# A fused attention kernel on one core: first scores on 256 tokens, keys ahead of values, a longer ring at first, and output weights loaded in pieces

## The chip, the cores and the metric

The kernel runs on one core of one Trainium2 chip. The metric is the device time of one execution in microseconds (us). A profiled execution gives a trace, whose span is about 1 to 2 us shorter than the time. Short names of the engines: PE is TensorE (matmuls), PEld its weight loads, ACT is ScalarE, DVE is VectorE, POOL is GpSimd, SP is SyncE, which issues most DMAs here.

## The reference

Two attention blocks over 2048 tokens, width 1024, 32 heads of 32. Their outputs stand side by side.

```python
# A: softmax attention
q, k, v = split(A_x @ A_wqkv)                       # 32 heads x 2048 x 32
p = softmax(q @ k.T * 32 ** -0.5)                   # 2048 x 2048 for each head
a = (p @ v) @ A_wo
# B: four segments of 512 tokens; in a segment causal attention, mixed by a gate
# with a linear-attention memory M, z of the segments before
p = softmax(qs @ ks.T * scale + mask);  a_dot = p @ vs
a_mem = (phi(qs) @ M) / (phi(qs) @ z + 1e-6)
o = g * a_mem + (1 - g) * a_dot
M, z = M + phi(ks).T @ vs, z + sum(phi(ks))
b = o @ B_wo
return concatenate([a, b], -1)
```

## The kernel before

Everything is laid out at build time. A small list scheduler keeps its own estimate of the time of each engine, and emits instructions in the order in which it believes them to become ready. The order is then fixed: at run time each engine executes its list in order and waits on semaphores. The names that matter here:

- An **exponential** is one ACT instruction over 128 x 1024 scores (4 heads x 256 queries x 2 tiles of 128 keys make two of them). There are 1216.
- The **ring** PT holds exponentials until PE has multiplied them with V (**PV**) and with ones (the row sums).
- **Side work** of PE: projections of Q, K, V for the next heads, B's memory, output projections.
- **Filler matmuls**: while the scheduler's clock is under WARM = 60 us, it puts a dummy matmul wherever it sees PE idle for 0.15 us.

```python
SLOTS = [(0, 1), (2, 3), (4, 5)]     # PSUM banks of scores
RING = 20
PACE = 240                           # how early the projections of the next heads are made
WARM = 60
TURNS = 2                            # chunks of 512 tokens of x that PE transposes; the others by DMA
...
    def loads(self):
        for k in range(4 * TURNS):
            tile_in(k)               # 128 tokens of A's x, from the SP queue
            ...                      # the three weights go between
        for c in range(TURNS, 4):    # chunks 2 and 3: DMA transpose
            R.dma(... self.A_x[0][512 * c:512 * c + 512, :], transpose=True ...)
...
    def a_prep(self, g):             # K, Q, V of four heads
        for c in range(4):
            yield pace()
            yield from proj(0, c)                      # K of 512 tokens
            if early and c == 0:
                yield from proj(1, 0)                  # Q of 512 tokens
                self.events.add(("sA", g, 0))          # scores may start
                self.spawn(values(), (-1, 1.5), "valuesA0")    # V, between the keys
        ...
    def emit_pv(self, u, st, part):
        for ones in (False, True):
            for h in range(4):
                ...
...
            if now < WARM and gap >= 0.15:             # filler
                ...
                R.op("PE", lambda e, bank=spare[0]: e.matmul(self.ps[:, bank, :], self.ones[:, :], ...), cost=MM)
```

## Time and profile before

| | us |
|---|---|
| time, median of 3 runs (range) | 1177.57 (1177.24 to 1180.48) |
| span of the profiled run | 1177.4 |
| ACT busy | 1125.4 (96%) |
| of that, 1216 exponentials | 1103.2, so 0.907 each |
| PE busy | 1028.4 (87%) |

From the page of the kernel before: the busy time of each engine, then shares of 40 equal slices in tenths (PEclk is the granted TensorE clock, also in tenths), and the costliest group.

```profile
PE 1028.4 (87%) x16647; PEld 480.5 (41%) x16880; DVE 800.1 (68%) x1367; ACT 1125.4 (96%) x1256; POOL 116.1 (10%) x192
...
ACT  4899999999999999998999999999999999999994
...
PEclk9999999999999998997999999999999999899998
...
L538 ACT ACTIVATE PT<-ps 128x1024 bf16<-128x1024 f32 (+1 forms) x1216 | 1103.2, 1037 | 29.4 <-PE ps L512 27.2
```

ACT is full everywhere but in the first slices and the last. The clock row has 7s and 8s in the middle; the prediction below counts them as dips that may "fall elsewhere" and gives them no cause.

ACT's timeline of the kernel before (start, duration, engine, line, what, count, idle time before it and what ended that):

```profile
5.90 1.02 ACT L425 ACTIVATE xA<-ps 128x1024 bf16<-128x1024 bf16 x1 [3.62 <-PE ps L420]
8.95 1.02 ACT L425 ACTIVATE xA<-ps 128x1024 bf16<-128x1024 bf16 x1 [2.03 <-DVE xA L427]
16.44 7.49 ACT L538 ACTIVATE PT<-ps 128x1024 bf16<-128x1024 f32 x8 [6.46 <-PE ps L512]
25.69 1.94 ACT L538 ACTIVATE PT<-ps 128x1024 bf16<-128x1024 f32 x2 [1.76 <-PE ps L512]
28.63 1.94 ACT L538 ACTIVATE PT<-ps 128x1024 bf16<-128x1024 f32 x2 [1.00 <-PE ps L512]
32.43 2.85 ACT L538 ACTIVATE PT<-ps 128x1024 bf16<-128x1024 f32 x3 [1.86 <-PE ps L512]
...
40.60 18.52 ACT L538 ACTIVATE PT<-ps 128x1024 bf16<-128x1024 f32 x20 [1.65 <-PE ps L512]
```

The first exponential starts at 16.44 us; 18 are done at 40.6 us, where 24 more microseconds of work would have fitted. From then on ACT hardly pauses.

### The profile page before, as it was taken

To read this page: it belongs to the slowest core of one execution; us is meant where nothing else is said; L and a number is where in the kernel's file an instruction comes from. 1 tells how busy PE (TensorE), PEld (TensorE's weight loads), DVE (VectorE), ACT (ScalarE), POOL (GpSimd) and SP (SyncE) were. 2 spreads that over 40 slices of the span, in tenths; PEclk is the share of its full clock that TensorE was granted. 3 is DMA by queue.
4 is the path that set the end of the run, shared out by engine and by line. 5 is a ranking of instruction groups with operands and counts; after the bars stand their busy time and mean duration, and the time that the engine had idled before them with its cause. 6 is when DMAs were issued, how large, how long until landed. Compare 5 with 4: busy or idle time off the path is not lost.

```text
span 1177.4 us, 36953 instructions
## 1 busy us (share of the span) xinstructions
PE 1028.4 (87%) x16647; PEld 480.5 (41%) x16880; DVE 800.1 (68%) x1367; ACT 1125.4 (96%) x1256; POOL 116.1 (10%) x192
## 2 busy tenths in 40 slices
PE   8988988998898978888989887888998989799995
PEld 4444434443344434333444433434443434344442
DVE  4367477668877468768787777875868887854345
ACT  4899999999999999998999999999999999999994
POOL 1001010011111011102011111110111120200000
PEclk9999999999999998997999999999999999899998
DMA  7752133152311221411311123120131211200111
GB/s 170 149 123 47 33 73 67 41 109 42 73 28 33 56 51 38 82 38 28 73 51 34 33 56 68 29 55 20 42 70 33 51 42 29 82 28 20 38 38 66
DMA packets 203272, 65.92 MB, mean 56 GB/s; under 512 B 195938, under 2 KB 195938, under 8 KB 203106
## 3 DMA queue, kind: packets, MB, share of 16 engines
q1 hardware_dynamic: 203106, 63.46, 24.0%
q8 instruction: 134, 2.20, 0.8%
q14 instruction: 32, 0.26, 0.1%
HBM read 37.75 MB, written 8.39 MB: 39 GB/s over the span
## 4 chain that ended last, share of the span: by engine, by line
ACT 48%; PE 41%; DVE 7%; issue 2%; DMA 0%; SPq 0%; another core or an unknown queue 0%; DVEq 0%
ACT PT L538 46%; PE ps L685 22%; PE ps L587 11%; PE ps L512 8%; DVE SQ L610 2%; DVE OL L597 1%; ACT E L878 1%; DVE OL L645 0%; DMA OTA<-in_A_x_dram 0%; DVE amem L912 0%; DVE outsb L981 0%; DVE OTA L614 0%; DVE KQB L695 0%; DVE KA L695 0%; SPq L383 0%
## 5 line engine op out<-in xcount | busy, mean ns | idle before, releaser
L538 ACT ACTIVATE PT<-ps 128x1024 bf16<-128x1024 f32 (+1 forms) x1216 | 1103.2, 1037 | 29.4 <-PE ps L512 27.2
L587 PE MATMUL ps<-PT,ones 128*32 128x256 bf16 x4864 | 293.7, 275 | 0.0
L587 PE MATMUL ps<-PT,VA 128*32 128x256 bf16 x4096 | 252.8, 279 | 14.8 <-ACT PT L538 10.4
L512 PE MATMUL ps<-QA,KA 32*128 32x256 bf16 x4096 | 209.3, 277 | 43.6 <-ACT PT L538 37.1
L610 DVE RECIPROCAL SQ<-OL 128x128 f32<-128x128 f32 x256 | 242.8, 949 | 5.0
L685 PE MATMUL ps<-xB,WB 128*128 128x512 bf16 x689 | 177.1, 381 | 25.2 <-issue 11.2
L685 PE MATMUL ps<-xA,WA 128*128 128x512 bf16 x689 | 181.2, 389 | 15.3 <-issue 9.4
L558 POOL TENSOR_SCALAR_AFFINE_SELECT PT<-PT 128x512 bf16<-128x512 bf16 x128 | 85.1, 667 | 909.9 <-ACT PT L538 905.3
L512 PEld LDWEIGHTS ps<-QA,KA 32*128 32x128 bf16 x4096 | 61.6, 92 | 223.8 <-ACT PT L538 205.4
L587 PEld LDWEIGHTS ps<-PT,VA 128*32 128x32 bf16 x4096 | 109.0, 96 | 104.6 <-issue 66.2
L587 PEld LDWEIGHTS ps<-PT,ones 128*32 128x32 bf16 x4864 | 131.7, 98 | 2.8
L597 DVE COPY OL<-ps 128x512 f32<-128x512 f32 x128 | 85.7, 669 | 25.2 <-PE ps L587 23.7
L685 PEld LDWEIGHTS ps<-xB,WB 128*128 128x128 bf16 x768 | 62.2, 97 | 98.5 <-issue 46.4
L685 PEld LDWEIGHTS ps<-xA,WA 128*128 128x128 bf16 x768 | 63.4, 99 | 91.4 <-issue 29.8
L905 DVE RECIPROCAL den<-den 128x128 f32<-128x128 f32 x96 | 91.1, 949 | 2.1
L984 DVE CAST outsb<-ps 128x512 bf16<-128x512 f32 x56 | 38.5, 687 | 74.5 <-PE ps L685 74.4
L695 DVE CAST KQB<-ps 128x512 bf16<-128x512 f32 x64 | 43.6, 681 | 53.5 <-PE ps L685 53.0
L685 PE MATMUL ps<-xA,OTA 128*128 128x512 bf16 x231 | 61.0, 391 | 4.1 <-issue 3.8
L685 PE MATMUL ps<-WoB,OTB 128*128 128x512 bf16 x228 | 57.9, 380 | 7.4 <-issue 3.6
L645 DVE SCALAR_TENSOR_TENSOR OL<-OL,SQ 128x256 f32<-128x256 f32 x128 | 59.1, 462 | 4.4
L587 PE MATMUL ps<-PT,VB 128*32 128x256 bf16 (+1 forms) x768 | 48.0, 270 | 13.7 <-DVE OL L597 9.9
L695 DVE CAST QA<-ps 128x512 bf16<-128x512 f32 x32 | 22.1, 691 | 42.9 <-PE ps L685 42.6
(69 smaller groups left out, 488.2 us busy)
## 6 DMA issues: line engine op xcount, KB each, us to landing
WB<-in_B_wk_dram SPq DMA_DIRECT2D x32, 256.0 KB, 2.9
WB<-in_B_wq_dram SPq DMA_DIRECT2D x32, 256.0 KB, 2.9
WB<-in_B_wv_dram SPq DMA_DIRECT2D x32, 256.0 KB, 3.1
out_dram<-outsb SPq DMA_DIRECT2D x32, 256.0 KB, 2.0
WA<-in_A_wqkv_dram SPq DMA_DIRECT2D x24, 256.0 KB, 3.7
OTA<-in_A_x_dram SPq DMA_DIRECT2D x8, 256.0 KB, 4.9
WoB<-in_B_wo_dram SPq DMA_DIRECT2D x1, 2048.0 KB, 10.7
xA<-in_A_wo_dram SPq DMA_DIRECT2D x1, 2048.0 KB, 9.6
```

The costliest lines, as they stand in the source:

```text
L512: ins = e.matmul(o, l, r, start=True, stop=True)
L538: op = R.op("ACT", lambda e: e.activation(self.PT[:, s0:s0 + n, 0:width], self.ps[:, banks[0]:banks[0] + n, 0:width], ACTF.Exp, bias=cb, s ...
L558: mo = R.op("POOL", lambda e, ap=ap, pat=pat: e.affine_select(ap, ap, pattern=pat, compare_op=ALU.is_ge, fill=0.0, base=0, channel_multipl ...
L587: ins = e.matmul(o, l, r, start=start, stop=end, skip_group_check=True)
L597: R.op("DVE", lambda e: e.tensor_copy(self.OL[x][:, :], self.ps[:, OLB, :]), r=[("ps", OLB)], w=[("OL", x)], cost=0.66)
L610: R.op("DVE", lambda e, cs=cs: e.reciprocal(rec[:, cs], L[:, cs]), r=[ko], w=[k], cost=0.93)
L645: R.op("DVE", lambda e: e.scalar_tensor_tensor(L, L, 1.0, rec, ALU.mult, ALU.add, accum_out=self.rng[:, u.seq:u.seq + 1]), r=[k, ko], w=[k ...
L685: ins = e.matmul(o, l, rh, start=a, stop=z)
L695: op = self.R.op("DVE", lambda e: e.tensor_copy(dst, self.ps[:, bank, :]), r=[("ps", bank)], w=[dkey], cost=0.66)
L878: ex = R.op("ACT", lambda e: e.activation(self.E[:, k0:k1, :], KQ[:, k0:k1, :], ACTF.Exp), r=[("KQB", b, k) for k in range(k0, k1)], w=["E ...
L905: R.op("DVE", lambda e, cs=cs: e.reciprocal(self.den[:, cs], self.den[:, cs]), r=["den"], w=["den"], cost=0.9)
L984: op = R.op("DVE", lambda e, ns=ns, bank=bank, ob=ob: e.tensor_copy(self.outsb[ob][:, ns], self.ps[:, bank, :]), r=[("ps", bank)], w=[("ou ...
```

## The change

Its intent is to start ACT earlier. Four things are done for it:

1. Only the first 512 tokens of x are transposed by PE, the other 1536 by DMA. The first loads come from two queues, SP and ACT. K and Q of the first 256 tokens are made first, so that scores can start.
2. All K of the first heads come ahead of V. The exponentials must wait for their PV, so the ring has 52 places at first: 20 of PT, 16 in the still empty tile of B's output weights (WoB), 16 in B's output tiles (OTB).
3. Wo of B (which now can be loaded only after the ring is short again) and Wo of A come in eight pieces.
4. The scheduler's constants are retuned. PACE goes from 240 to 220; the estimates of DMA times change.

```diff
-PACE = 240
+PACE = 220
 WARM = 60
-TURNS = 2
+TILES = (0, 1, 2, 3)
+LONG = 52
+UNTIL = 100
...
+        tile_in(0, "SP")
+        tile_in(1, "ACT")
+        self.load_WA(0, 0, "SP")
+        self.load_WA(1, 0, "ACT")
+        tile_in(2, "SP")
+        tile_in(3, "ACT")
...
+        for c in range(4):
+            if 4 * c not in TILES:
+                turned(c)
+        self.load_WA(2, 0, "ACT")
...
+        if early:
+            for kind, c, h in ((0, 0, (0,)), (1, 0, (0,)), (0, 0, (1,)), (0, 1, (0, 1)), (0, 2, (0, 1)), (0, 3, (0, 1)), (1, 0, (1,))):
+                ...
+                yield from proj(kind, c, h)
+            for c in range(4):
+                if c == QNEXT:
+                    yield from proj(1, 1, (0,))
+                yield from proj_V(c)
...
+    def pt(self, i, n):                       # place i of the ring
+        if i < RING:
+            return self.PT[:, i:i + n, :]
+        i -= RING
+        if i < 16:
+            return self.WoB[...]
+        return self.OTB[(i - 16) // 8][...]
...
-        if self.ring + n > RING:
+        if self.ring + n > self.ring_len:
             self.ring = 0
+            if self.posA >= UNTIL:
+                self.shorten()                # back to 20 places
...
+        for j in range(NG):
+            yield ("pos", 128 + 16 * j)
+            self.R.dma(lambda e, j=j: e.dma_start(self.WoB[:, j, :], self.B_wo[P * j:P * j + P, :]), ...)
```

## The prediction

> **What bounds it now.** The page has ScalarE (ACT) busy 1125.4 of 1177.4 us (96%), PE 87%. 1216 exponentials fill 1103.2 us, 0.907 us each (busy time over count). The change leaves them alone, so only ACT idle time can be won, and most lies at the start. In ACT's timeline the first exponential starts at 16.44 us; pauses of 1.76, 1.00, 1.86 and 1.65 us follow; from 40.6 us ACT is full. By then 18 are done, 16.7 us of work: 24 us lost. From 60 to 1160 us ACT's waits sum to 14.4 us, mostly where the table by stage shows a granted clock of 0.84 to 0.96. After the last exponential (1161.3) comes a tail of 16 us.
>
> The start is slow because the first scores need 512 tokens of K and Q. The tile that completes them lands at 9.5 us (DMA step in the chain of waits); turns, K and Q projections (1.7 us each) and a cast follow. Then PE makes V and PV between the keys, so the last K chunk is cast only at 31.25 us.
>
> **What the change does.**
> - 256 tokens first: two tiles and two weights, from two queues. The Trainium skill ("Trainium Kernel Development and Optimization", Key Constraints) says that queues share the 16 DMA engines, only issue time is saved; the profile agrees that transfers limit here (DMA share about 0.9 to 1.2 from 2 to 10 us). 1 MB at some 290 GB/s, shared with other loads, lands at 6 to 8 us. Turns, two half-width projections (0.9 us each, estimated) and casts put the first exponential at about 10 us (9 to 12).
> - Three chunks by DMA transpose, not two. Each held the SP queue 5.77 us and landed 1.7 to 3 us after that. From 2.1 us on, they should land near 10, 15.5 and 21 us.
> - Keys first, ring of 52: the last K chunk no longer waits for V and PV. Exponentials 13 to 16 need it: 21 + projection 1.8 + cast 0.7 + scores 0.4, about 24.2 us. 12 (11.1 us) are then done: 13 us lost, not 24. The last chunk thus decides, not the first exponential.
> - Deferred PV (about 8 steps of 0.9 us) is paid back from PE's 13% slack; cost to ACT 0 to 2 us.
> - Two x copies (1.02 us) leave ACT, five DMA issues (0.45 us) come, all before its first exponential: free.
> - Wo of B in eight pieces instead of 2 MB at 54 us, Wo of A likewise: 0 to 1 us (ACT loses 0.9 us from 60 to 100 us).
> - Compiled order of the tail nearly the same: 1 us either way.
>
> **Sum.** 11 us at the start, less 1 to 2 us for payback: 1177.6 - 9.6 = 1168.0 us, ratio 0.992. Range 1162.5 to 1173.5 (8 in 10). Faster by over 2% needs the whole start removed: 0.02. Within 2%: 0.97. Slower: 0.01.
>
> **What would show it.** ACT's timeline: first exponential near 10 us, pauses before the 5th, 9th and 13th, the 13th near 24 us, about 28 done at 40 us. DMA issues: three transposes, 5.8 us apart. ACT busy unchanged within 3 us; the span shorter by the ACT idle time saved in the first 40 us. Idle from 60 us on near 14 us, tail near 16 us.
>
> **What would make it wrong.** The first transpose, beside tiles and weights, delays them or takes longer (gain 5 us or less). PE overloaded from 25 to 80 us by late V and PV beside B's preparation. Dips of the granted clock that fall elsewhere. A rearranged middle that loses or wins a few us.

## The result, and the profile after

Ratios here are the mean time of one kernel's runs over that of the other's runs of the same rounds, so not quite the ratio of the medians quoted.

The changed kernel took 1178.55 us (median of 4, 1176.75 to 1179.46) against 1177.4 us before: ratio 1.0003, 95% interval 0.9982 to 1.0024. The change moved nothing that can be told from noise, and lies outside the predicted range.

The page and ACT's timeline of the changed kernel:

```profile
PE 1069.7 (91%) x16874; PEld 480.1 (41%) x16874; DVE 795.6 (68%) x1368; ACT 1123.4 (95%) x1254; POOL 114.3 (10%) x192
...
ACT  5999999999999999999999998989999999999993
...
PEclk9999999999999998989999998989999998999998
```

```profile
12.12 1.94 ACT L584 ACTIVATE PT<-ps 128x1024 bf16<-128x1024 f32 x2 [7.25 <-PE ps L544]
...
16.55 1.94 ACT L584 ACTIVATE PT<-ps 128x1024 bf16<-128x1024 f32 x2 [1.48 <-PE ps L544]
19.56 5.61 ACT L584 ACTIVATE PT<-ps 128x1024 bf16<-128x1024 f32 x6 [1.08 <-PE ps L544]
...
27.77 5.61 ACT L584 ACTIVATE WoB<-ps 128x1024 bf16<-128x1024 f32 x6 [0.77 <-PE ps L544]
33.21 7.52 ACT L584 ACTIVATE OTB<-ps 128x1024 bf16<-128x1024 f32 x8
40.62 9.49 ACT L584 ACTIVATE PT<-ps 128x1024 bf16<-128x1024 f32 x10
```

The start did improve: the first exponential is at 12.12 us, and 26 instead of 18 are done at 40.7 us. (PE's larger busy time is no more work: of the kernel before, 16647 matmuls but 16880 weight loads are on record, so some matmul records are missing. The missing 233 are all matmuls of 512 columns. In the changed kernel's trace none is missing, and PE is busy 91% there; so PE's real slack is nearer 9% than the 13% that the prediction reads from the page before.)

So the gain was won and lost again. To see where, I counted exponentials in both traces. The table gives the start of the n-th.

| exponential | 1 | 13 | 61 | 301 | 651 | 741 | 851 | 951 | 1051 | last ends | span |
|---|---|---|---|---|---|---|---|---|---|---|---|
| before | 16.44 | 32.43 | 79.65 | 301.01 | 634.60 | 717.94 | 823.49 | 914.84 | 1006.43 | 1161.33 | 1177.4 |
| after | 12.12 | 27.77 | 72.01 | 295.67 | 625.35 | 709.18 | 817.59 | 910.45 | 1004.98 | 1159.63 | 1177.7 |
| lead of after | 4.3 | 4.7 | 7.6 | 5.3 | 9.3 | 8.8 | 5.9 | 4.4 | 1.5 | 1.7 | -0.3 |

The lead of 7.6 us at the 61st exponential is still there at the 741st, though it was 5.3 us at the 301st. It then shrinks to 1.7 us at the last one, and the tail after it takes 2.0 us more. The tables by stage of both kernels show how (window, its length, then the busy time of PE, PEld, DVE, ACT and POOL with the number of instructions, the mean granted clock, the DMA share and GB/s). First the kernel before:

```profile
400.00:700.00 300.00, 258.80 (x4259) 119.56 (x4320) 218.85 (x364) 292.85 (x326) 33.76 (x54) 0.95 0.23 50
700.00:1060.00 360.00, 311.49 (x5202) 145.79 (x5267) 271.51 (x461) 354.28 (x398) 40.46 (x64) 0.97 0.20 46
```

The changed kernel:

```profile
400.00:700.00 300.00, 269.39 (x4363) 120.21 (x4361) 213.77 (x359) 294.96 (x327) 29.70 (x48) 0.97 0.23 50
700.00:1060.00 360.00, 320.01 (x5126) 142.48 (x5126) 269.45 (x456) 346.79 (x390) 44.24 (x70) 0.95 0.19 43
```

From 700 to 1060 us ACT (fourth number after the length) is busy 346.8 us where it was 354.3, 7.5 us less, and the granted clock is 0.95 where it was 0.97. The clock records of the traces have only two values, 1.0 and 0.5. I call an interval at 0.5 a **dip**. Each dip before the last exponential is a multiple of 3.41 us long; the table counts these (a last stretch at 0.5, in the tail, lies in both traces). ACT idle time sorted by dips (a dip and the 3 us after it), with what is left elsewhere after 60 us:

| | dips | us at half clock | ACT idle in dips | ACT idle elsewhere, 60 us to the last exponential | span after the last exponential |
|---|---|---|---|---|---|
| before | 9 | 58.0 | 11.8 | 4.7 | 16.1 |
| after | 8 | 54.6 | 14.2 | 7.6 | 18.1 |

Start -7.6, dips +2.4, elsewhere +2.9, tail +2.0: the sum is -0.3 where the spans differ by +0.3, so 0.6 us are not placed. Four separate terms cancel.

### The profile page after: what moved, and what is told of

Same layout as the page of the kernel before. It is cut to its first block, busy times and chain, and to the rows that moved or that the text cites. A ratio compares the mean times of both kernels' runs of the same rounds, so it can differ in the third digit from the quotient of the medians.

```text
span 1177.7 us, 37192 instructions
## 1 busy us (share of the span) xinstructions
PE 1069.7 (91%) x16874; PEld 480.1 (41%) x16874; DVE 795.6 (68%) x1368; ACT 1123.4 (95%) x1254; POOL 114.3 (10%) x192
## 3 DMA queue, kind: packets, MB, share of 16 engines
q1 hardware_dynamic: 204512, 62.41, 23.6%
## 4 chain that ended last, share of the span: by engine, by line
ACT 49%; PE 43%; DVE 6%; issue 1%; DMA 1%; DVEq 0%
ACT PT L584 47%; PE ps L731 23%; PE ps L633 11%; PE ps L544 8%; DVE SQ L656 2%; DVE OL L643 1%; ACT E L921 1%; DVE OL L691 0%; ACT WoB L584 0%; DMA OTA<-in_A_x_dram 0%; DVE outsb L1025 0%; DVE KQB L741 0%; DVE OL L682 0%; DVE KA L741 0%; DVE OTA L660 0%
## 5 line engine op out<-in xcount | busy, mean ns | idle before, releaser
L584 ACT ACTIVATE PT<-ps 128x1024 bf16<-128x1024 f32 (+1 forms) x1184 | 1074.0, 1043 | 31.7 <-PE ps L544 30.1
L633 PE MATMUL ps<-PT,ones 128*32 128x256 bf16 (+1 forms) x4736 | 285.7, 274 | 0.0
L633 PE MATMUL ps<-PT,VA 128*32 128x256 bf16 x3968 | 244.4, 278 | 17.5 <-ACT PT L584 9.9
L731 PE MATMUL ps<-xA,WA 128*128 128x512 bf16 (+1 forms) x792 | 200.7, 387 | 4.0 <-DVE amem L955 1.0
L731 PE MATMUL ps<-xB,WB 128*128 128x512 bf16 x768 | 195.0, 382 | 7.2 <-DVE den L941 3.6
L633 PEld LDWEIGHTS ps<-PT,VA 128*32 128x32 bf16 x3968 | 105.4, 96 | 108.0 <-issue 65.1
L633 PEld LDWEIGHTS ps<-PT,ones 128*32 128x32 bf16 x4736 | 128.0, 98 | 2.5
L731 PE MATMUL ps<-WoB,OTB 128*128 128x512 bf16 x256 | 64.6, 382 | 2.0 <-DVE OTB L684 0.8
L731 PE MATMUL ps<-xA,OTA 128*128 128x512 bf16 x256 | 65.8, 388 | 0.1
L741 DVE CAST VT<-ps 128x512 bf16<-128x512 f32 x32 | 21.9, 685 | 44.7 <-PE ps L731 44.7
```

Of the source, the lines that this page charges most:

```text
L584: op = R.op("ACT", lambda e: e.activation(self.pt(s0, n)[:, :, 0:width], self.ps[:, banks[0]:banks[0] + n, 0:width], ACTF.Exp, bias=cb, sc ...
L633: ins = e.matmul(o, l, r, start=start, stop=end, skip_group_check=True)
L731: ins = e.matmul(o, l, rh, start=a, stop=z)
L741: op = self.R.op("DVE", lambda e: e.tensor_copy(dst, self.ps[:, bank, 0:n]), r=[("ps", bank)], w=dkeys, cost=0.12 + n * 0.00105)
```

## The experiments

Theory G: the gain of the start is real and lies on the critical path; the newly compiled order gives it back later. Rival P: the total is set by PE's work under the throttle of its clock, so starting earlier only brings more idle time later. Later came theory H, on what the dips are, and its rival L. One difference decides how much a run proves. The runs a_again, a_delay, a_light, b_light and a_tail keep the compiled order of their kernel: in the traces the weight loads, VectorE and ACT instructions follow in the same sequence, but for those added or cut. In a_warm, b_warm, the runs with another ring and those with another pace the scheduler arranges the whole order anew.

### The same kernel again

No edit.

> The changed kernel unedited, for a second trace and a firmer time. Theory G (the head gain of 7.3 us is real and later parts of the new order give it back): ratio 0.998 to 1.002; the waits on VectorE near 210, 793 and 1034 us and the 1.9 us pause among the last waits of the SP queue recur at the same instructions, because the order is compiled in. Theory P (the total is fixed by PE work under the clock throttle): same ratio, half-speed time again 50 to 60 us, but the pauses outside the dips need not recur.

Measured: 1178.48 us, ratio 0.9989 (0.9970 to 1.0007). Eight dips again, 58.0 us, seven of them within 5 us of the same place as in the first trace (for example 521.5, 702.4, 729.7, 763.9, 982.3, 1016.5 against 522.4, 703.4, 730.7, 764.8, 983.2, 1017.4 us, in a run that is 0.6 to 1.2 us ahead at the 61st to the 741st, the 951st and the 1051st exponential). ACT idle in dips 13.4 us, elsewhere 7.57 us (7.59), span after the last exponential 18.2 us (18.1). So the dips, the waits and the tail belong to the compiled order. That speaks for G: dips that recur at the same places are no chance disturbance.

### ACT delayed

```diff
         R.op("ACT", lambda e: e.activation(self.gcol[:, 0, :], self.PT[:, RING - 1, 0:8], ACTF.Exp), ...)
+        for _ in range(36 if not self.shifted else 0):
+            R.op("ACT", lambda e: e.activation(self.den[:, :], self.PT[:, RING - 1, :], ACTF.Exp), r=[("PT", RING - 1)], w=["den"], cost=0.0)
```

> The changed kernel with 36 dummy activations ahead of its first exponential, some 12 us more of ACT start; the compiled order is otherwise the same on every engine. By the traces this should put exponentials at 60 us back by some 7 us. Theory G: the span grows by as much as the count of exponentials at 60 us falls behind, about 6 to 8 us (ratio 1.005 to 1.007). Theory P: the lost time is made up later, growth of 0 to 2 us.

Measured: 1198.22 us, ratio 1.0149 (1.0126 to 1.0173). The 61st exponential started at 89.82 us, 17.8 us later than in the changed kernel, and the last one ended 19.1 us later. So a loss at the start, with the order unchanged, passes through to the end in full: P is wrong, and the start lies on the critical path, as G says. My figure for the delay itself was far off (6 to 8 us). The reason stands in the stages of this run:

```profile
13.00:16.30 3.30, 1.67 (x11) 0.81 (x11) 0.45 (x1) 3.14 (x6) 0.00 (x0) 1.00 1.21 263
16.30:19.70 3.40, 0.00 (x0) 0.00 (x0) 0.00 (x0) 3.24 (x6) 0.00 (x0) 1.00 1.05 228
19.70:36.70 17.00, 4.14 (x16) 1.17 (x16) 1.39 (x5) 12.71 (x22) 0.00 (x0) 0.50 0.11 24
```

PE had nothing to do from 16.3 to 19.7 us, because ACT was blocked (PE busy is the first number after the length: 0.00). The clock fell to 0.50 right at the end of that window, and stayed there for 17 us, in which PE remained mostly idle and then made the first projections at half speed.

### PE lightened, both kernels

```diff
-        for ones in (False, True):
+        for ones in (False, True) if st == 0 and part == 0 else (False,):
             for h in range(4):
```

The results are wrong on purpose.

> The changed kernel with the row-sum matmuls cut to the first of each unit (wrong result on purpose), same order, some 250 us less PE work. Both: hardly any ACT idle time in dips of the clock, 1150 to 1160 us. The pair with b_light tells: theory P (PE and throttle eat the gain): a_light shorter than b_light by the head gain, 6 to 8 us. Theory G with losses fixed in the new order and tail: shorter by only 1 to 4 us.

> The kernel before with the same cut. 1158 to 1165 us; ACT idle time in dips near zero. See a_light for what each theory expects of the difference.

Measured: a_light 1170.78 us (ratio to the kernel before 0.9921, 0.9899 to 0.9943), b_light 1182.77 us (1.0024, 1.0002 to 1.0046). Both expectations fell. With some 4350 matmuls fewer, the kernel before became no faster. Half-clock time rose from 54.6 to 95.6 us in the changed kernel and from 58.0 to 116.1 us in the kernel before, ACT idle time in b_light's dips from 11.8 to 23.7 us. (a_light's dips cost ACT no more than the changed kernel's, 13.4 us after 14.2, and a_light took 0.8% less than the kernel before. That it leads b_light by 12 us fits neither theory's figure.) The rows of the granted clock of a_light and then of b_light:

```profile
PEclk9999999999999987989999997899998998899997
```

```profile
PEclk9999999999999978998999998899999989799998
```

Less PE work gave more dips. So these dips are not a throttle against too much work.

The Trainium skill ("TensorE: Matmul & The Clock Gate", Part 1: The HAM clock gate) describes just such a gate: half clock is the resting state, an idle window of about 3.4 us on a free-running grid leads to it, and a busy window leads out of it. The traces agree on the two values, on the 3.41 us (all dips are multiples of it), and on the direction. They say more about how busy is busy enough. I laid the grid of each trace's clock records over its matmuls. In the four traces of before, after, a_again and a_pace240 (below), the 32 full-clock windows that a dip follows had PE busy between 37% and 61% of the time. Of the 1252 windows without one, up to the last exponential, all but four had 57% or more. So a window need not be idle: of the 35 windows under 56.5%, 31 were followed by a dip. The limit is not sharper than that (the four had 46 to 54%; three of them are in the trace of the kernel before, where matmul records are missing). A dip ended after a window at half clock with PE busy 72% or more, mostly above 90%.

For a dip of the changed kernel:

```profile
444.00:447.40 3.40, 1.89 (x41) 0.79 (x41) 1.95 (x4) 3.40 (x5) 0.00 (x0) 1.00 0.00 0
447.40:450.80 3.40, 1.42 (x40) 0.69 (x40) 3.30 (x5) 3.40 (x6) 1.44 (x3) 1.00 0.00 0
450.80:461.00 10.20, 8.62 (x111) 3.48 (x104) 7.91 (x13) 9.00 (x11) 3.80 (x6) 0.50 0.01 2
461.00:464.40 3.40, 3.30 (x42) 1.20 (x40) 2.83 (x6) 2.62 (x4) 0.00 (x0) 1.00 0.03 5
```

Up to 450.8 us ACT is full (3.40 of 3.40) and PE has too little to do: 1.42 of 3.40 us, 42%. At half clock the same work fills PE, ACT then goes short (9.00 of 10.20, and 2.62 of 3.40 after). This is theory H: the engine off the critical path is so idle that its clock is halved, and then it becomes the critical one. Its cure is not less PE work but more.

### Fillers throughout, both kernels

```diff
-WARM = 60
+WARM = 1150
```

> The changed kernel with the filler matmuls that it has until 60 us allowed until 1150 us wherever the scheduler sees PE idle for 0.15 us. Theory H (dips of the clock follow stretches in which PE was too little busy, so they belong to the compiled order): most of the 55 to 58 us at half clock vanish, ACT idle time in dips falls from 13 to 14 us to under 5 us, the time by 6 to 10 us (ratio 0.992 to 0.995). Rival L (dips come from too much PE work): more dips, ratio 1.00 to 1.01.

> The same for the kernel before. Theory H: ACT idle time in dips from 11.8 to under 5 us, ratio 0.993 to 0.996. With the dips gone in both, a_warm should be 2 to 4 us shorter than b_warm: the head gain of 7.6 us less 2.9 us of VectorE waits and 2 us of tail that stay.

Measured: a_warm 1167.06 us (ratio 0.9894, 0.9872 to 0.9916), b_warm 1171.86 us (0.9937, 0.9915 to 0.9959). Half-clock time fell to 6.8 and 3.4 us, ACT idle time in dips to 3.9 and 1.4 us. The rows of the clock, a_warm and then b_warm, and the stage of 700 to 1060 us of a_warm, where ACT is busy 355.68 us instead of the changed kernel's 346.79:

```profile
PEclk9999999999999999999999999999999999999998
```

```profile
PEclk9999999999999999999999999999999999999998
```

```profile
700.00:1060.00 360.00, 326.83 (x5274) 149.20 (x5351) 273.04 (x461) 355.68 (x399) 39.80 (x64) 1.00 0.18 42
```

This is what H expects: with 169 and 181 fillers in place of 16 and 14, both kernels are faster, by 1.1% and 0.6%. One reservation belongs here. The scheduler reckons with the fillers and so compiles another order too. But in the five orders that were compiled with fillers until 1150 us there are 0 to 2 dips, and in the five without (all PE work kept) 7 to 10; so it is the fillers, and not one lucky order, that remove the dips. And with the dips gone the gain of the change appears: a_warm leads b_warm by 8.2 us at the 61st exponential and by 6.9 us at the end of the last. In the time, 4.8 us of it are left. The rest went into a_warm's tail, 22.1 us where b_warm has 19.6. Of these 2.5 us, 2.2 are a pause among SP's last waits that b_warm lacks (next section); the outputs themselves end only 0.6 us later after the last exponential (15.1 and 14.5 us), though 40 output matmuls were left after the last scores, in b_warm 27.

### The last waits of SP

The tail of the changed kernel is 2.0 us longer, though the last DVE group ends only 0.4 us later after the last exponential (11.4 us, where it was 11.0). First this group before, then after:

```profile
1169.83 2.48 DVE L981 TENSOR_TENSOR outsb<-ps,xB 128x512 bf16<-128x512 f32 x4 [0.29 <-PE ps L685]
```

```profile
1168.51 2.48 DVE L1025 TENSOR_TENSOR outsb<-ps,xB 128x512 bf16<-128x512 f32 x4 [0.29 <-PE ps L731]
```

Among the 12 waits with which SP ends, the trace of the changed kernel has a pause: the third starts at 1174.82 us, the fourth at 1176.73; in the kernel before, all follow each other within 0.08 us. I put four satisfied waits ahead of them:

```diff
                 fast.play(eng, name)
+                for _ in range(4 if name == "SP" else 0):
+                    eng.wait_ge(fast.sem["DVE"], 1)
```

> The changed kernel with four waits that are already satisfied put into the SP queue ahead of the last branch, which moves all later SP instructions. If the 1.9 us pause among the last waits of SP is the fetch of instructions at a boundary, it moves or goes, and the span after the last exponential falls from 18.1 to about 16.2 us; if it is a wait for an output transfer, it stays. The whole time: about 2 us less (0.998) or the same.

Measured: 1178.67 us, ratio 1.0002 (0.9972 to 1.0033); span after the last exponential 19.0 us. The pause did not go, it moved: now it lies after the first wait (1172.55 to 1174.79 us) instead of after the third. The four waits are on record as two instructions, and the pause lies just two instructions earlier. A pause that shifts with the number of instructions ahead of it is not a wait for an output. The reading that fits is that SP waits for the next stretch of its own instructions. (An 8 KB transfer of the DMA kind "instruction" starts inside the pause, at 1175.25 us; but in the kernel before one starts just as late after the first wait, 0.6 us, without a pause, so it alone shows nothing.) That the pause costs the changed kernel 1.9 us and the kernel before nothing is luck of where the boundary fell. It matters for the pairs here: a pause of 1.9 to 2.3 us is in the traces of the changed kernel, a_again, a_delay, a_light, a_tail, a_warm, a_pace240 and a_warm240 (the last two below), and in no trace of the kernel before or its variants, nor in the runs with the ring at 20.

### The ring at 20 places, without and with fillers

```diff
-LONG = 52
+LONG = 20
```

> The changed kernel with the ring at 20 places from the start. If the long ring is needed for the head gain, ACT loses some 5 us more before 60 us (PV must precede the keys) and the 61st exponential starts near 77 us instead of 72; if not, it starts within 1 us of 72 us. The rest of the order is rearranged, so the total may shift by a few us either way: 1174 to 1186 us.

> The changed kernel with fillers until 1150 us and the ring at 20 places from the start, against a_warm, which differs in the ring alone. With the dips gone in both, theory G (the start is on the critical path) expects the 61st exponential near 82 us as in a_ring20, against 71 us in a_warm, and most of these 11 us in the total: 1172 to 1178 us. A rival, that the rest of the order makes up for the start, expects 1165 to 1169 us.

Measured: a_ring20 1175.24 us (ratio 0.9970, 0.9941 to 0.9999), a_ring20_warm 1170.23 us (0.9919, 0.9891 to 0.9948). ACT's timeline of a_ring20 shows that the early start needs the ring: it stops after ten exponentials.

```profile
19.37 5.61 ACT L584 ACTIVATE PT<-ps 128x1024 bf16<-128x1024 f32 x6 [1.07 <-PE ps L544]
32.69 7.44 ACT L584 ACTIVATE PT<-ps 128x1024 bf16<-128x1024 f32 x8 [7.71 <-PE ps L544]
```

The 61st exponential started at 82.29 us, 10.3 us later than in the changed kernel. My 77 us was missed too. Yet the total is no worse, rather better, because this order has 8.2 us of ACT idle time in dips (14.2), 3.3 us elsewhere (7.6), and 13.1 us of tail (18.1; 1.9 of the difference is SP's pause). So 10 us were lost at the start, and more than that was won by another order. The total of one order says little about a start. With fillers the pair differs by 11.0 us at the 61st exponential (81.97 against 70.98), 7.5 us at the end of the last one, and 3.2 us in the median time; I had expected most of the 11 us, and 1170.23 us lies between what the two theories expect. The first 3.5 us went mostly in pauses of ACT after 60 us (9.8 us in a_warm, 6.0 here), the next part into the tail, 16.3 us here and 22.1 us in a_warm: 2.2 of it is SP's pause, 4.1 that the outputs end later after the last exponential. So a gain of the start can shrink without dips as well; why the rest of these two orders differs was not tested.

### The pace constant

The prediction passed over PACE, the one part of the change that acts on the middle.

```diff
-PACE = 220
+PACE = 240        # a_pace240, a_warm240; in b_pace220, b_warm220 the kernel before gets 220
```

> The changed kernel with the pace constant of the projections back at 240. The head is compiled the same, so the 61st exponential should start within 1 us of 72 us; dips and tail are arranged anew. Theory H with luck of the order: total anywhere from 1172 to 1183 us, with the difference to the changed kernel found in dips, VectorE waits and tail. If the constant itself was what gave the gain back: 1170 us or less.

> The kernel before with the pace constant of the change. The head stays (61st exponential within 1 us of 79.7 us); total within 5 us of the kernel before, either way, by dips and tail.

> The changed kernel with fillers until 1150 us and the pace constant at 240. If the constant acts through the dips, within 2 us of a_warm's 1167 us. If through the order and the tail, 1162 to 1165 us. The dips should be as few as in a_warm (under 15 us at half clock).

> The kernel before with fillers until 1150 us and the pace constant at 220. Acts through dips: within 2 us of b_warm's 1172 us. Through order and tail: 1174 to 1178 us. Against a_warm at the same pace of 220 the head gain of 7.6 us should show, less what the tails differ by: 4 to 9 us longer than a_warm.

| pace | before | changed | before, fillers | changed, fillers |
|---|---|---|---|---|
| 240 | 1177.3 to 1180.4 | 1175.40 (0.9958, 0.9928 to 0.9988) | 1171.86 (0.9937) | 1165.92 (0.9891, 0.9871 to 0.9911) |
| 220 | 1185.18 (1.0048, 1.0019 to 1.0077) | 1178.55 and 1178.48 (1.0003, 0.9989) | 1169.75 (0.9925, 0.9907 to 0.9943) | 1167.06 (0.9894) |

(Medians, ratio to the kernel before of the same rounds. The kernel before is given as the range of its medians.)

The start is unmoved by the constant: 71.73 us for the 61st exponential in a_pace240, 79.23 us in b_pace220. Without fillers 220 costs the kernel before 0.5%, and the changed kernel probably about 0.4% (the intervals overlap a little). With fillers it costs neither: 0.9925 against 0.9937, 0.9894 against 0.9891. So what the constant costs comes through the dips: in the trace of a_pace240 half-clock time is 34.1 us, where the changed kernel has 54.6, and ACT idle in dips 8.7 us, where it has 14.2; ACT idle elsewhere is rather more, 9.7 us after 7.6. With two values of the constant tried, it is not shown whether 220 is worse as such or only happens to give orders with more dips. (The traced run of b_pace220, 1180.61 us, was the fastest of four, the others 1185.0 to 1187.7, so its dips are not set against the median.) At equal pace and without fillers the rest of the change is worth about 0.4% at 240 and 0.5% at 220: 5 to 6 us of the 7.6. With fillers it is 0.5% at 240 and 0.3% at 220; b_warm220 was 2.7 us longer than a_warm, where I had expected 4 to 9. In each of these pairs the changed kernel has SP's pause of about 2 us and the other has not.

### A version that beats both

a_best is a_warm with a third buffer for output rows in the tail (B's tile E, no longer used there), and eight extra waits that move SP's instruction boundary. a_best240 has the pace of 240 as well.

```diff
-WARM = 60
+WARM = 1150
+        self.outsb.append(self.E[:, :, :].rearrange("p a b -> p (a b)"))
...
             if u.g == NG - 1:
+                if u.c == 0:
+                    self.out_free.append(2)
...
-                  r=[("ps", bank)], w=[("outsb", ob, half)], cost=0.66)
+                  r=[("ps", bank)], w=[("outsb", ob, half)] + ["E"] * (ob == 2), cost=0.66)
...
+                for _ in range(8 if name == "SP" else 0):
+                    eng.wait_ge(fast.sem["DVE"], 1)
```

> a_warm with a third buffer for output rows at the end (a tile of the B part that is no longer used) and the SP queue's instructions moved further. The two waits for output transfers in a_warm's tail (2.0 us each) go, and the pause of 2.2 us among the last SP waits goes or moves into the branch before it: 1161 to 1165 us, ratio 0.985 to 0.988 to the kernel before.

> a_best (fillers, third output buffer at the end, SP instructions moved) with the pace constant at 240; its compiled tail has 11 and 12 output matmuls after the last scores where a_best has 8, 16 and 16. 1159 to 1164 us, ratio 0.983 to 0.987.

Measured: a_best 1164.85 us (0.9873, 0.9848 to 0.9898). The pause of SP is gone (its waits run from 1164.35 to 1165.03 us without one), but the tail is 23.6 us. The third buffer did not shorten it: 40 output matmuls were still behind the last scores, PE fell to half clock in it (16 of them took 5.33 us, 16 earlier ones 3.63), and the chain of waits has 4.27 us for a transfer out of the third buffer. a_best240 took 1160.99 us, 0.9853 (0.9832 to 0.9874) of the kernel before; its tail is 18.0 us. Here the third buffer did help. a_warm240 has the same order of weight loads and 27 output matmuls left as well, but a tail of 23.3 us: 2.3 us of SP's pause, a wait of 2.0 us for an output transfer in its chain that a_best240 lacks, and the last DVE group ends 16.1 us after the last exponential instead of 12.5. a_best240 gives correct results, and is 1.5% faster than the kernel before and about as much faster than the changed one.

## Why the prediction was wrong, point by point

- **What bounds the kernel: right.** ACT bounds it. a_delay shows that a loss at the start passes to the end, 17.8 us to 19.1.
- **"11 us at the start": right mechanism, size off.** It was 7.6 us at the 61st exponential. The first exponential was put "at about 10 us", and came at 12.12; the 13th "about 24.2 us", and came at 27.77; "about 28 done at 40 us" were 26. The two tiles (4.56 and 4.88 us) and the two weights (6.05 and 6.98 us) landed as estimated. But the second tile was turned and copied only at 7.98 us, K's projection begins at 8.12 us, and the two half-width projections took 3.03 us, where 0.9 each was estimated. Two queues did not make x land sooner (the first two tiles before, both from SP, landed at 3.51 and 4.14 us), as the remark of the Trainium skill that the prediction cites ("Trainium Kernel Development and Optimization", Key Constraints) would have it. The 13th exponential needs the third transpose; that landed at 22.99 us, 2 us later than the "near 21" forecast. And the order, compiled for an earlier start, put scores that had to wait for ACT ahead of the last K projection, as PE's timeline after shows:

```profile
22.89 0.82 PE L1230 MATMUL ps<-ones 128*128 128x512 bf16 x3
24.31 0.40 PE L544 MATMUL ps<-QA,KA 32*128 32x256 bf16 x8 [0.59 <-ACT PT L584]
24.64 1.90 PE L731 MATMUL ps<-xA,WA 128*128 128x512 bf16 x8
```

  The projection begins at 24.64 us, 1.65 us after the landing, behind fillers and the waiting scores. That these 1.65 us are due to the order was argued, not tested.
- **Three transposes 5.8 us apart: right in the mean only** (16.89 us of issue for three). The first, beside tiles and weights, held the queue 8.55 us, a risk that the prediction names; the others took 3.92 and 4.33. They landed at 13.42, 17.65 and 22.99 us, where "near 10, 15.5 and 21" was forecast.
- **"Idle from 60 us on near 14 us": this is the step that failed.** It was 21.8 us (14.2 in dips and 7.6 elsewhere; counted so, 16.4 before). By the prediction's own count, the sum of ACT's waits, 14.4 us became 20.3. The lines are of the kernel before and of the changed one, from 60 to 1162 us:

```profile
ACT PT L538 <- PE ps L512: 14.4, 25, 2.0
ACT PT L584 <- PE ps L544: 20.3, 25, 2.1
```

  I took the dips of the clock for an outside disturbance, which would "fall elsewhere". The runs showed that they are made by the compiled order: a window of 3.41 us with PE under some 55 to 60% busy mostly brings one. The prediction also counted PE's 13% slack as free, to pay back the deferred PV. That slack was not free: bunched into such windows, it was followed by half clock.
- **"A rearranged middle that loses or wins a few us" was named as a risk, but priced at zero.** It cost 5.3 us (2.4 in dips, 2.9 elsewhere), of which the overlooked PACE is probably 3 to 5: by so much a_pace240 is faster (0.9958 against 1.0003 and 0.9989).
- **"Compiled order of the tail nearly the same: 1 us either way": for the engines right, for the tail not.** 24 output matmuls instead of 16 were left after the last scores, which moved the last DVE group by 0.4 us. But the tail grew from 16.1 to 18.1 us, 1.9 of it by the pause among SP's last waits, which no list of the engines' order shows.
- **Payback of PV "0 to 2 us": right.** ACT loses about 1.0 us from 60 to 100 us in both.
- **Wo in pieces** was not tested alone. Between 60 and 100 us the idle time of both traces is alike, so no gain of it is seen.

Left open: why this order leaves PE idle at these very places; and the 2.9 us elsewhere. The largest three of them in the changed kernel (1.63 us near 210, 1.37 near 793, 0.96 near 1034 us) have PE's list waiting for a DVE copy with scores behind it, and recur in a_again, but none was taken away by itself.

## What to carry to other kernels

Where one engine bounds and PE follows it with slack, look at PE's busy share in windows of 3.4 us. Here windows under about 57% were mostly followed by half clock, just before PE was needed again, and dummy matmuls in the gaps were worth more than the shorter start. A change to a kernel whose order is compiled by a scheduler changes the whole order; compare the lead at fixed points of the work (here the n-th exponential), not only the total, and test a retuned constant by itself. Before believing that a change "does nothing", see whether its gain is there in the stage it was made for.

## What the Trainium skill lacked or had wrong

- "TensorE: Matmul & The Clock Gate", Part 1, has the clock halved after an idle window. It also tells of a kernel whose clock swung because PE paused often and briefly, but gives no busy share at which that begins. Here the windows ahead of dips were not idle: PE was busy 37 to 61% of them (32 windows in four traces), and nearly all windows above 57% kept the full clock. In this kernel, which another engine bounds, ACT was idle 12 to 14 us of 1177 in such dips (before, after and a_again).
- The same page says that a busy window restores the clock. Here windows at half clock with PE busy 53 to 86% of the time did not always do it; the ones that ended a dip were at 72 to 100%. A stretch of sparse work was kept at half clock for up to 20.5 us (b_light).
- The same page advises to avoid idle gaps; that filler matmuls in the gaps pay in a kernel bound by another engine (ratio 0.989 and 0.994) stands on no page that I read.
- "Runtime: NRT & Kernel Launch", Instruction fetch mechanics, is the page for the loading of an engine's own instructions, but it gives no length of a pause. Here pauses of 1.9 to 2.3 us stood among SP's last waits and moved when instructions were added ahead of them; that they are such a loading is the reading that fits, not shown.
